# Two decode layers on one core: last wo and w2 blocks turned at once, sum of squares later, w3 as 3 and 2 rows, four V pages by halves of partitions

## The chip, the cores and the metric

The kernel runs on one core of a Trainium2 chip. The metric is the device time of one execution in microseconds (us), lower is better. A run of the program is timed several times; the median of the runs is the time that is compared.

## The reference

One token goes through attention and a gated feed-forward block, and through both once more with the same weights and the same caches. Each of the two passes is called a layer here.

```python
def _layernorm(x, eps=1e-5):               # no scale, no bias
    return (x - mean(x)) / sqrt(var(x) + eps)

def _A_ref(x, k_cache, v_cache, wq, wo):   # x: 1x1x640, caches: 32 heads x 32768 x 192, bf16
    W = min(4096, max(256, Sk // 4))       # 4096: the last 4096 positions are used
    q = (x @ wq) as 32 heads x 192
    p = softmax(q . k[last W] * 192 ** -0.5)
    return (p . v[last W]) @ wo            # wo: 6144x640

def _B_ref(x, w1, w3, w2):                 # w1, w3: 640x1536, w2: 1536x640
    return (silu(x @ w1) * (x @ w3)) @ w2

x = x + _A_ref(_layernorm(x), ...)
x = x + _B_ref(_layernorm(x), ...)
x = x + _A_ref(_layernorm(x), ...)
x = x + _B_ref(_layernorm(x), ...)
```

A head's 4096 x 192 keys are 1536 KB, its values as much, and there are 32 heads. A layer's caches and weights are over 100 MB, so nearly all of the work is to bring them in.

## The kernel before

All loads go out from SyncE (SP), in one order that the list `loads` (lines 192 to 235) sets down: for each layer wq in pieces, then pages of K and V by turns (V six heads behind K), then wo, w1, w3 and w2. Their destination is the `arena`, 32 units of 128 partitions x 3072 bf16 columns; a K or V page takes two units (128 partitions x 12288 bytes). `refill()` (lines 250 to 273) issues loads from the head of the list as long as `place()` finds free units; `done(key)` (line 289) frees the units of a page whose last reader has been written down, and refills. So the order of the program fixes which instruction a load waits for: the last reader of the units that it takes. The scheduler keeps eight semaphores for DMAs and takes them in turn, so a load also waits until the load eight places before it has landed. Three buffers lie outside the arena: `wo5` (the last 2560 columns of layer 0's wo), `keep` (the last 2400 of w2's 7680 columns, kept for layer 1) and `rest`.

Thirteen heads' K pages (`RETAIN`) stay in the arena from layer 0 to layer 1 and one more is parked in PSUM, so layer 1 loads fewer, and at the passage between the layers few units are free. There wq comes in ten pieces of 3072 columns, each of which can go out only when units are freed.

TensorE (PE) does the products with the weights, K or V as the moving operand; since x is one row, the stationary operand is narrow (32 columns for q, w1 and w3, one column for wo and w2). VectorE (DVE) turns each K page in blocks of 32x32 (line 379), finds the maxima of the softmax and sums; ScalarE (ACT) takes exponentials and copies.

The functions that the change touches, with their part in the order of work:

- `layernorm()` (lines 296 to 307): squares x on DVE, sums x and its squares by two fp32 products with a matrix of 1/640 (an fp32 product stands as two records on PE), subtracts the mean into `xs`, the stationary operand of what follows; the standard deviation's reciprocal `rstd` comes by Ln and Exp on ACT and is used only when a result is copied out of PSUM.
- `y_to_residual()` (309 to 319): the output of wo or w2 stands in PSUM as four partial rows of 640; ACT and DVE copy a half each to SBUF as `y_sb`, five products with `y_sb` as stationary operand turn and add them into a column per 128 elements, and DVE adds them to x (`xsq[:, 0:5]`).
- `wo_proj()` (491 to 521) multiplies blocks of 640 columns of wo (two matmuls of 320 columns) by one column of `otd`; `ffn()` (532 to 585) does w1, `gate()`, w3, the product and, in layer 0, w2 by blocks of 640 columns with a column of `htd`; `last_rows()` (587 to 598) does w2 in layer 1, straight into four rows of the output.
- `softmax_place()` (420 to 432) puts the turned probabilities of a block of four heads in place and forms the reciprocal of their sum; `combine()` (448 to 464) folds the block's output and scales it.
- `out_open()` and `out_residual()` (473 to 489) put x itself into the output's rows by five fp32 products.

A value is ready for the next part thus, at the passage from layer 0 to layer 1: last columns of w2 land in `keep`; their matmuls; both casts; five products; the residual; two fp32 sums; the subtraction; the first piece of wq; `done` of that piece, and with it the next load.

Of the kernel before, what the change touches and what calls it, by code (L numbers as in the profile page):

```python
# [8 lines left out]
F32 = mybir.dt.float32  # L9
# [6 lines left out]
P = 128  # L16
D = 640
# [23 lines left out]
SPLIT = (("k", 12),)  # L41
KW = 4 * HB
WH = 6 * KW + 32 - KW
KEEP = 2400
W2A = 2880
# [8 lines left out]
def kernel(  # L54
# [38 lines left out]
    onesD, rl, st, nv, lnv, rstd, l = (sc[:, a:b] for a, b in ((0, 1), (1, 2), (2, 4), (4, 5), (5, 6), (6, 7), (7, 8)))  # L93
# [8 lines left out]
    nc.vector.memset(xs[:].rearrange("p c n -> p (c n)").bitcast(U32), 0)  # L102
# [85 lines left out]

    def units_of(width):
        return -(-width // U)  # L190

    for layer in range(2):
# [3 lines left out]
        for i in range(H + LEAD):  # L196
            kinds = (("v", i - LEAD, A_v_cache), ("k", i, A_k_cache))
            for kind, g, cache in kinds[::-1] if k_first(layer, i) else kinds:
# [8 lines left out]
                if layer == 1 and (kind, h) in SPLIT:  # L207
                    for th in range(2):
                        loads.append(((kind, layer, h, th), 1, [(0, U, src[:, U * th:U * th + U])]))
                else:  # L210
                    loads.append(((kind, layer, h), 2, [(0, PGW, src)]))
        for key, ranges in wo_units(layer):
# [4 lines left out]
            if key:  # L217
                loads.append((key, units_of(at), parts))
            else:
                dst = wo5 if at == 2560 else wo4  # L220
                loads.append((None, None if dst is wo5 else LAST, [(dst[:, o:o + n], src) for o, n, src in parts]))
        if layer == 0:
# [7 lines left out]
            loads.append((None, None, [(keep[:], w2_v[:, 7680 - KEEP:7680])]))  # L230
        else:
            loads.append((("fa", layer), units_of(7680), [(0, 7680, w1_v[:, 0:7680])]))
            loads.append((("fb", layer), 2, [(0, PGW, w3_v[:, 0:PGW])]))
            loads.append((("fc", layer), 1, [(0, 1536, w3_v[:, PGW:])]))
# [15 lines left out]
    def refill():  # L250
        while loads:
# [18 lines left out]
            for off, w, src in parts:  # L270
                pin(nc.sync.dma_start(out=arena[:, s * U + off:s * U + off + w], in_=src))  # L271
# [24 lines left out]
    def layernorm():  # L296
        pin(nc.vector.tensor_tensor(out=xsq[:, 6:6 + NCH], in0=xsq[:, 0:NCH], in1=xsq[:, 0:NCH], op=ALU.mult))
        st_ps = m_ps[:, 0:12]
        for g in range(2):
            mm(st_ps[:, 6 * g:6 * g + 6], lhsT=onesD.broadcast_to([P, P]), rhs=xsq[:, 6 * g:6 * g + 6], start=True, stop=True)  # L300
        pin(nc.vector.reduce_sum(out=st[:, 0:1], in_=st_ps[:, 0:6], axis=AX.X))
        pin(nc.vector.tensor_scalar(out=xs[:, :, 3], in0=xsq[:, 0:NCH], scalar1=st[:, 0:1], scalar2=None, op0=ALU.subtract))
        pin(nc.vector.reduce_sum(out=st[:, 1:2], in_=st_ps[:, 6:12], axis=AX.X))
        pin(nc.vector.scalar_tensor_tensor(out=nv[:], in0=st[:, 0:1], scalar=st[:, 0:1], in1=st[:, 1:2],
                                           op0=ALU.mult, op1=ALU.subtract))
        pin(nc.scalar.activation(out=lnv[:], in_=nv[:], func=ACTF.Ln, scale=-1.0))
        pin(nc.scalar.activation(out=rstd[:], in_=lnv[:], func=ACTF.Exp, scale=-0.5))

    def y_to_residual(y_ps, f_ps=None):
# [4 lines left out]
        for c in range(NCH):  # L314
            mm(yt_ps[:, c:c + 1], lhsT=y_sb[:, c:D:NCH], rhs=onesb, start=True, stop=True)
# [22 lines left out]
    def q_turn(f0, f1, late):  # L338
# [7 lines left out]
        for a in range(4):  # L346
            dst = _ap(qt_sb[:], 0, 32, 96 * f0 + 2 * a, [[8, 2], [1, 2], [16, ns]])
            src = qt_ps[32 * a:32 * a + 32]
            eng = nc.vector if a % 2 and not late else nc.scalar
            pin((eng.copy if eng is nc.scalar else eng.tensor_copy)(out=dst, in_=src))  # L350
# [50 lines left out]
    def softmax_head(b, s_ps):  # L401
# [3 lines left out]
        for th in range(2):  # L405
# [9 lines left out]
                                 accum_out=l[0:64]))  # L415
# [4 lines left out]
    def softmax_place(b, et):  # L420
        engs = [nc.scalar, nc.vector, nc.scalar, nc.vector, nc.scalar, nc.vector, nc.scalar, nc.scalar]
        for th in range(2):
# [5 lines left out]
        half = slice(64 * (b % 2), 64 * (b % 2) + 64)  # L428
        rl_ps = m_ps[:, 0:1]
        mm(rl_ps[half], lhsT=lt[0:64], rhs=l[0:64], start=True, stop=True,  # L430
           tile_position=(0, 64 * (b % 2)))
        pin(nc.vector.reciprocal(out=rl[half], in_=rl_ps[half]))  # L432
# [15 lines left out]
    def combine(b, o_ps):  # L448
        half = slice(64 * (b % 2), 64 * (b % 2) + 64)
# [3 lines left out]
        ot_ps = m_ps.rearrange("p (q e) -> p q e", q=16)  # L453
        for par in range(2):
            mm(ot_ps[half].rearrange("p q e -> p (q e)"), lhsT=sel[:, par, :, :].rearrange("p h q -> p (h q)"),
               rhs=o_sb[:, 192 * par:192 * par + 192], start=(par == 0), stop=(par == 1),
               tile_position=(0, 64 * (b % 2)))
        om = w20[half, 384:576].rearrange("p (q e) -> p q e", q=16)
        pin(nc.vector.scalar_tensor_tensor(out=om, in0=ot_ps[half], scalar=rl[half],  # L459
                                           in1=mask[half].unsqueeze(2).broadcast_to([64, 16, 12]),  # L460
                                           op0=ALU.mult, op1=ALU.mult))
        with nc.allow_low_precision("one nonzero term in each sum"):
            pin(nc.vector.reduce_sum(out=otd[half, 12 * pos:12 * pos + 12], in_=om.rearrange("p q e -> p e q"),
                                     axis=AX.X))
# [8 lines left out]
    def out_open():  # L473
        assert not loads
        spare = free[0] * U
        ident = arena[:, spare:spare + 64].bitcast(F32)
        nc.gpsimd.memset(ident, 0.0)
# [3 lines left out]
        xw = arena[:, spare + 64:spare + 64 + 1280].bitcast(F32)  # L481
        nc.gpsimd.memset(xw, 0.0)
        for j in range(4):
            nc.gpsimd.tensor_copy(out=xw[32 * j:32 * j + 32, 32 * j:640:128], in_=xsq[32 * j:32 * j + 32, 0:NCH])
        return pss[:, 0:160], xw, ident

    def out_residual(f_ps, xw, ident):
        for c in range(NCH):
            mm(f_ps[:, c:160:NCH], lhsT=xw[:, 128 * c:128 * c + 128], rhs=ident, start=(c == 0), stop=False)

    def wo_proj(layer):
# [6 lines left out]
        for key, ranges in turns:  # L498
            at, width = 0, wo_width(ranges)
            for pos, lo, hi in ranges:  # L500
                x = lo
# [18 lines left out]
        y_to_residual(y_ps, last and last[0])  # L520
# [11 lines left out]
    def ffn(layer, f_ps):  # L532
# [20 lines left out]
        else:  # L553
            steps = ((g_ps, "fa", 0, 5, 0), (u_ps, "fb", 0, 4, 0), (u_ps, "fc", 4, 5, 0))
# [136 lines left out]
```

## Time and profile before

| what | value |
|---|---|
| median of three runs | 526.64 us (526.46 to 527.17) |
| profiled execution, device time | 525.68 us |
| profiled execution, span from first to last instruction | 523.7 us |
| mean granted clock of TensorE | 0.699 |
| bytes read | 219.74 MB, 420 GB/s over the span |
| busy share of the span: PE, DVE, ACT, POOL | 55%, 49%, 13%, 4% |
| loads of V pages | 64 of 1536 KB |
| loads of K pages of full width | 49 of 1536 KB |

"Span" is the time between the first and the last instruction of one profiled execution; the device time of the same execution holds some 2 us more. A row of the chain of waits says when a piece of the chain starts, how long it lasts, and which engine, tile and line it belongs to; "issue" is time in which an engine waited for nothing that the profile shows. Matmuls all stand at line 86, a helper, and are told apart by the tile that they write: q_ps, s_ps and o_ps in attention, y_ps for wo and w2, g_ps and u_ps for w1 and w3, pss for the small ones. In the busy windows a row gives a stretch of time, its length, each engine's busy time with the number of instructions, the granted clock, the share of the DMA engines' time and the rate.

### The profile page before, as it was taken

How to read it: one execution, taken by the hardware profiler on the slowest of the kernel's cores; microseconds unless marked ns; L12 is line 12 of the kernel's file. 1: busy time of each engine (PE TensorE's matmuls, PEld its weight loads, DVE VectorE, ACT ScalarE, POOL GpSimd, SP SyncE). 2: the span in 40 equal slices, each digit the busy share in tenths (PEclk: the TensorE clock that was granted, in tenths of full speed). 3: DMA queues.
4: the chain of work that ended last, by engine and by line, in shares of the span. 5: the costliest groups of instructions: out<-in, count | busy, mean ns of one | idle time of the engine just before them, and what ended most of it. 6: DMA issues, size and time to landing. Idle time of an engine off the chain costs nothing.

```text
span 523.7 us, 5996 instructions
## 1 busy us (share of the span) xinstructions
PE 286.0 (55%) x2396; PEld 111.3 (21%) x2396; DVE 255.8 (49%) x385; ACT 66.0 (13%) x202; POOL 19.1 (4%) x86
## 2 busy tenths in 40 slices
PE   3335555463655544655555685676356565365564
PEld 1101222121222111212112231232112222122132
DVE  0079885656746476763002117431678565565002
ACT  1010210110202020202001022121201120112000
POOL 4010000000000000000000001000000000001000
PEclk9967778675776768666555577788557867776567
DMA  9999999999999999999999999999999999999996
GB/s 376 406 432 428 428 431 428 429 429 429 429 430 428 431 429 427 430 429 429 424 420 403 388 412 433 428 426 431 426 432 430 426 432 426 431 431 427 431 428 251
DMA packets 22931, 220.12 MB, mean 420 GB/s; under 512 B 2680, under 2 KB 3064, under 8 KB 7288
## 3 DMA queue, kind: packets, MB, share of 16 engines
q1 hardware_dynamic: 22760, 219.75, 99.2%
q8 instruction: 19, 0.31, 0.2%
q14 instruction: 8, 0.07, 0.0%
q10 hardware_dynamic: 144, 0.00, 0.0%
HBM read 219.74 MB, written 0.00 MB: 420 GB/s over the span
## 4 chain that ended last, share of the span: by engine, by line
DMA 84%; PE 10%; DVE 3%; issue 1%; ACT 1%; SPq 1%; DVEq 0%; ACTq 0%
DMA arena<-in_A_k_cache_dram 47%; DMA arena<-in_A_v_cache_dram 24%; DMA arena<-in_B_w_dram 6%; PE s_ps L86 5%; PE o_ps L86 2%; DVE arena L379 2%; DMA arena<-in_A_wo_dram 2%; DMA keep<-in_B_w_dram 2%; DMA arena<-in_A_wq_dram 1%; DMA wo<-in_A_wo_dram 1%; PE q_ps L86 1%; PE pss L86 1%; SPq L271 1%; PE u_ps L86 0%; PE y_ps L86 0%
## 5 line engine op out<-in xcount | busy, mean ns | idle before, releaser
L86 PE MATMUL s_ps<-arena,wst 128*16 128x512 bf16 (+1 forms) x768 | 157.7, 524 | 157.4 <-DVE arena L379 80.7
L379 DVE STREAM_TRANSPOSE arena<-arena 128x1536 uint32<-128x1536 uint32 x100 | 171.1, 1753 | 67.0 <-DMA arena<-in_A_k_cache_dram 66.5
L86 PE MATMUL o_ps<-arena,ptm 128*8 128x384 bf16 (+1 forms) x1024 | 115.2, 438 | 24.0 <-DMA arena<-in_A_v_cache_dram 24.0
L86 PEld LDWEIGHTS <-wst 128*16 128x16 bf16 (+1 forms) x768 | 48.9, 108 | 248.3 <-issue 216.1
L86 PEld LDWEIGHTS <-ptm 128*8 128x8 bf16 (+1 forms) x1030 | 40.7, 102 | 65.1 <-issue 53.4
L411 ACT ACTIVATE nt<-m 32x16 f32<-32x16 f32 x16 | 3.4, 213 | 271.4 <-DVE m L408 271.4
L427 ACT COPY ptm<-w 32x64 bf16<-32x64 bf16 x80 | 23.6, 295 | 46.5 <-PE o_ps L86 44.2
L86 PE MATMUL q_ps<-arena,xs 128*32 128x512 bf16 x120 | 19.2, 589 | 13.4 <-DMA arena<-in_A_wq_dram 12.3
L363 POOL COPY wst<-qt_sb 32x24 bf16<-32x24 bf16 x30 | 8.4, 280 | 422.9 <-PE s_ps L86 307.1
L459 DVE SCALAR_TENSOR_TENSOR w<-pss,sc,cb 64x192 bf16<-64x192 f32 x16 | 6.7, 416 | 33.5 <-PE pss L86 33.5
L402 DVE TENSOR_REDUCE lt<-s_ps 64x1 f32<-64x512 f32 x16 | 10.9, 684 | 23.0 <-PE s_ps L86 22.6
L86 PE MATMUL y_ps<-arena,otd 128*1 128x320 bf16 x176 | 15.3, 438 | 9.8 <-DMA arena<-in_A_wo_dram 9.3
L417 DVE STREAM_TRANSPOSE w<-w 64x512 bf16<-64x512 bf16 x16 | 11.3, 705 | 14.4 <-ACT w L414 14.4
L312 DVE CAST w<-y_ps 128x320 bf16<-128x320 f32 x3 | 1.5, 491 | 30.6 <-PE y_ps L86 30.6
L350 DVE CAST qt_sb<-pss 32x48 bf16<-32x48 f32 (+1 forms) x4 | 1.2, 307 | 28.6 <-ACT qt_sb L350 28.6
L86 PEld LDWEIGHTS <-xs 128*32 128x32 bf16 x200 | 8.3, 114 | 32.0 <-issue 25.2
L427 DVE COPY ptm<-w 32x64 bf16<-32x64 bf16 x48 | 10.0, 209 | 10.0 <-PE o_ps L86 8.9
L432 DVE RECIPROCAL sc<-pss 64x1 f32<-64x1 f32 x16 | 2.6, 165 | 23.1 <-PE pss L86 22.9
L452 ACT CAST w<-o_ps 128x384 bf16<-128x384 f32 x16 | 7.7, 479 | 31.8 <-PE o_ps L86 24.9
L414 ACT ACTIVATE w<-s_ps,nt 64x512 bf16<-64x512 f32 x16 | 10.9, 682 | 5.7 <-DVE nt L412 5.7
L86 PE MATMUL pss<-w,sel 128*64 128x192 bf16 x32 | 6.3, 286 | 8.1 <-ACT w L452 5.1
L86 PEld LDWEIGHTS <-otd 128*1 128x1 bf16 x192 | 5.8, 102 | 20.3 <-issue 15.8
(81 smaller groups left out, 119.2 us busy)
## 6 DMA issues: line engine op xcount, KB each, us to landing
arena<-in_A_v_cache_dram SPq DMA_DIRECT2D x64, 1536.0 KB, 29.2
arena<-in_A_k_cache_dram SPq DMA_DIRECT2D x49, 1536.0 KB, 29.2
arena<-in_A_wq_dram SPq DMA_DIRECT2D x10, 768.0 KB, 6.7
arena<-in_A_wq_dram SPq DMA_DIRECT2D x1, 4608.0 KB, 20.0
arena<-in_A_wo_dram SPq DMA_DIRECT2D x6, 720.0 KB, 8.7
arena<-in_A_wo_dram SPq DMA_DIRECT2D x2, 1920.0 KB, 30.1
arena<-in_A_wq_dram SPq DMA_DIRECT2D x2, 1536.0 KB, 7.7
arena<-in_B_w_dram SPq DMA_DIRECT2D x4, 768.0 KB, 7.1
```

What stands on the lines that cost most here:

```text
L86: return pin(nc.tensor.matmul(*a, **k))
L271: pin(nc.sync.dma_start(out=arena[:, s * U + off:s * U + off + w], in_=src))
L363: pin((engs[a].copy if engs[a] is nc.scalar else engs[a].tensor_copy)(out=dst, in_=src))
L379: pin(nc.vector.transpose(x, x))
L402: pin(nc.vector.reduce_max(out=t0[:, 0:1], in_=s_ps[0:64, :], axis=AX.X))
L411: pin(nc.scalar.mul(out=tb[32:64, 0:KW].rearrange("p (a z) -> p a z", a=4), in_=mb, mul=-SCALE))
L414: pin(nc.scalar.activation(out=e[:], in_=s_ps[0:64, :], func=ACTF.Exp, bias=nbt[:, 0:1], scale=SCALE, accum_out=l[0:64]))
L417: pin(nc.vector.transpose(et[:], e[:]))
L427: pin((eng.copy if eng is nc.scalar else eng.tensor_copy)(out=dst, in_=src))
L432: pin(nc.vector.reciprocal(out=rl[half], in_=rl_ps[half]))
L452: pin(nc.scalar.copy(out=o_sb[:, 0:384], in_=o_ps[:, 0:384]))
L459: pin(nc.vector.scalar_tensor_tensor(out=om, in0=ot_ps[half], scalar=rl[half], in1=mask[half].unsqueeze(2).broadcast_to([64, 16, 12]), op0 ...
```

## The change

- Layer 0's last 1920 columns of wo (`wo5`) and of w2 (`keep`) are three blocks of 640. They are no longer multiplied as the moving operand with a column of `otd` or `htd`, copied and turned. Each block itself, in five sets of 128 columns, is the stationary operand, and the column of `otd` or `htd` the moving one, so that the result is turned as it comes and adds to the same PSUM columns as the turned rest. The loads of `wo5` and `keep` are cut in three (`tail_cuts`): what lies ahead of the last two blocks in two transfers, and the last two blocks (1280 columns) in one.
- `layernorm()` does the sum of x and the subtraction, and returns `spread()`, which does the sum of squares and `rstd`; it is called after the first piece of wq, or after the first row of w1.
- Layer 1's w3 comes as 4608 and 3072 columns (3 and 2 of its 5 rows) in place of 6144 and 1536.
- Layer 1's V pages of heads 28 to 31, the last four, are loaded as two transfers each, of partitions 0 to 63 and 64 to 127 (`ROWS`).
- Fewer or other instructions: one sum and one reciprocal for two blocks of the softmax; `combine()` on partitions 0 to 63 for every block; all copies of the turned q on ACT; the copy of u on ACT in place of DVE; x into the output by one fp32 product of 160 columns in place of five of 32; the first memsets of `xs` and `wst` on GpSimd.

```diff
+ROWS = (28, 29, 30, 31)
+TAIL = 3 * 640
...
-    onesD, rl, st, nv, lnv, rstd, l = (sc[:, a:b] for a, b in ((0, 1), (1, 2), (2, 4), (4, 5), (5, 6), (6, 7), (7, 8)))
+    onesD, rl, st, nv, rstd, lnv, l = (sc[:, a:b] for a, b in ((0, 1), (1, 3), (3, 5), (7, 8), (5, 6), (6, 7), (6, 8)))
...
+    def tail_cuts(width):
+        return (0, width - TAIL), (width - TAIL, 640), (width - 1280, 1280)
...
-                    loads.append(((kind, layer, h), 2, [(0, PGW, src)]))
+                    parts = [(0, PGW, src)]
+                    if layer == 1 and kind == "v" and h in ROWS:
+                        parts = [(0, PGW, src[p0:p0 + 64], p0) for p0 in (0, 64)]
+                    loads.append(((kind, layer, h), 2, parts))
...
+                if dst is wo5:
+                    src = parts[0][2]
+                    parts = [(o, n, src[:, o:o + n]) for o, n in tail_cuts(2560)]
...
-            loads.append((None, None, [(keep[:], w2_v[:, 7680 - KEEP:7680])]))
+            loads.append((None, None, [(keep[:, o:o + n], w2_v[:, 7680 - KEEP + o:7680 - KEEP + o + n])
+                                       for o, n in tail_cuts(KEEP)]))
...
-            loads.append((("fb", layer), 2, [(0, PGW, w3_v[:, 0:PGW])]))
-            loads.append((("fc", layer), 1, [(0, 1536, w3_v[:, PGW:])]))
+            loads.append((("fb", layer), 2, [(0, 4608, w3_v[:, 0:4608])]))
+            loads.append((("fc", layer), 1, [(0, 3072, w3_v[:, 4608:])]))
...
-            for off, w, src in parts:
-                pin(nc.sync.dma_start(out=arena[:, s * U + off:s * U + off + w], in_=src))
+            for off, w, src, *at in parts:
+                p0 = at[0] if at else 0
+                pin(nc.sync.dma_start(out=arena[p0:p0 + src.shape[0], s * U + off:s * U + off + w], in_=src))
...
-        for g in range(2):
+
+        def total(g):
             mm(st_ps[:, 6 * g:6 * g + 6], lhsT=onesD.broadcast_to([P, P]), rhs=xsq[:, 6 * g:6 * g + 6], start=True, stop=True)
-        pin(nc.vector.reduce_sum(out=st[:, 0:1], in_=st_ps[:, 0:6], axis=AX.X))
+            pin(nc.vector.reduce_sum(out=st[:, g:g + 1], in_=st_ps[:, 6 * g:6 * g + 6], axis=AX.X))
+
+        total(0)
         pin(nc.vector.tensor_scalar(out=xs[:, :, 3], in0=xsq[:, 0:NCH], scalar1=st[:, 0:1], scalar2=None, op0=ALU.subtract))
...
+        def spread():
+            total(1)
...
+        return spread
...
-        for c in range(NCH):
-            mm(yt_ps[:, c:c + 1], lhsT=y_sb[:, c:D:NCH], rhs=onesb, start=True, stop=True)
+        turned_y = (lambda c: y_sb[:, c:D:NCH], onesb)
+        parts = [turned_y]
+        if tail:
+            w, hid, lo = tail
+            parts = [(lambda c, k=k: w[:, 640 * k + c:640 * k + 640:NCH], hid[:, lo + k:lo + k + 1]) for k in range(3)]
+            parts.insert(1, turned_y)
+            mm(yt_ps, lhsT=ptm[:, 2:3].broadcast_to([P, P]), rhs=ptm[:, 0:NCH], start=True, stop=False)
+        for n, (lhsT, rhs) in enumerate(parts):
+            for c in range(NCH):
+                mm(yt_ps[:, c:c + 1], lhsT=lhsT(c), rhs=rhs, start=not tail, stop=(not tail or (n, c) == (len(parts) - 1, NCH - 1)))
...
-        half = slice(64 * (b % 2), 64 * (b % 2) + 64)
-        rl_ps = m_ps[:, 0:1]
-        mm(rl_ps[half], lhsT=lt[0:64], rhs=l[0:64], start=True, stop=True,
-           tile_position=(0, 64 * (b % 2)))
-        pin(nc.vector.reciprocal(out=rl[half], in_=rl_ps[half]))
+        if b % 2:
+            rl_ps = m_ps[0:64, 0:2]
+            mm(rl_ps, lhsT=lt[0:64], rhs=l[0:64], start=True, stop=True)
+            pin(nc.vector.reciprocal(out=rl[0:64], in_=rl_ps))
...
-    def out_residual(f_ps, xw, ident):
-        for c in range(NCH):
-            mm(f_ps[:, c:160:NCH], lhsT=xw[:, 128 * c:128 * c + 128], rhs=ident, start=(c == 0), stop=False)
+    def out_residual(f_ps, xw, blk):
+        mm(f_ps, lhsT=blk, rhs=xw, start=True, stop=False)
...
-            steps = ((g_ps, "fa", 0, 5, 0), (u_ps, "fb", 0, 4, 0), (u_ps, "fc", 4, 5, 0))
+            steps = ((g_ps, "fa", 0, 5, 0), (u_ps, "fb", 0, 3, 0), (u_ps, "fc", 3, 5, 0))
...
+                if ps is g_ps and c == 0:
+                    spread()
...
-        pin(nc.vector.tensor_scalar(out=gu[:, 1, :], in0=u_ps[:, 0:384], scalar1=rstd, scalar2=None, op0=ALU.mult))
+        pin(nc.scalar.mul(out=gu[:, 1, :], in_=u_ps[:, 0:384], mul=rstd))
...
-        for fcx in range(12):
+        for fcx in range(9):
...
-        y_to_residual(y_ps)
+        y_to_residual(y_ps, None, (keep[:, KEEP - TAIL:], htd, 9))
...
             q_piece(layer, piece, q_ps)
+            if piece is now[0]:
+                spread()
```

## The prediction

> **What bounds the kernel now.** I read the 40 slices and the chain of waits on the page, then the busy windows by stage, then the chain in order of time at the two places that the change names.
>
> ```profile
> GB/s 376 406 432 428 428 431 428 429 429 429 429 430 428 431 429 427 430 429 429 424 420 403 388 412 433 428 426 431 426 432 430 426 432 426 431 431 427 431 428 251
> ...
> DMA 84%; PE 10%; DVE 3%; issue 1%; ACT 1%; SPq 1%; DVEq 0%; ACTq 0%
> ...
> arena<-in_A_v_cache_dram SPq DMA_DIRECT2D x64, 1536.0 KB, 29.2
> ```
>
> The DMA engines are busy in every slice, at 426 to 433 GB/s but for the start, slices 20 to 24 (the passage from layer 0 to layer 1) and the end. A page of K or V (1536 KB, 1.573 MB) therefore costs 1.573/0.430 = 3.66 us, and is issued 29.2 us ahead. The time is bytes over rate, plus the start, the dips and the tail; whatever lies beside the stream is free.
>
> ```profile
> 440.00:460.00 20.00, 9.70 (x73) 3.57 (x71) 11.39 (x14) 1.56 (x5) 0.56 (x2) 0.67 1.01 431
> ...
> 268.00:276.00 8.00, 4.55 (x50) 0.96 (x42) 0.00 (x0) 0.00 (x0) 0.00 (x0) 0.50 1.03 426
> ...
> 296.00:297.00 1.00, 0.97 (x8) 0.28 (x6) 0.00 (x0) 0.00 (x0) 0.00 (x0) 0.50 0.76 209
> 297.00:298.00 1.00, 0.39 (x2) 0.00 (x0) 0.00 (x0) 0.00 (x0) 0.00 (x0) 0.50 0.80 246
> ...
> 517.00:518.00 1.00, 1.00 (x17) 0.48 (x15) 0.40 (x2) 0.18 (x1) 0.00 (x0) 1.00 0.81 326
> 518.00:519.00 1.00, 0.47 (x6) 0.00 (x0) 0.66 (x3) 0.00 (x0) 0.00 (x0) 1.00 0.50 197
> 519.00:520.00 1.00, 0.53 (x23) 0.45 (x27) 0.32 (x2) 0.00 (x0) 0.00 (x0) 1.00 0.19 72
> ```
>
> The columns are the stretch, its length, busy time of PE, PEld, DVE, ACT and POOL, the granted clock, the DMA share and GB/s. Two things are to be seen. At 296 to 298 the stream runs dry: (425-209)+(425-246) = 395 GB/s-us, or 395/425 = 0.93 us lost. And at the end the rate fades over three microseconds: the 16 DMA engines, each with 1/16 of the bytes, do not finish together but over some 2.5 us.
>
> ```profile
> 290.86 0.77 PE y_ps L86 x8
> 291.63 0.02 issue
> 291.65 0.50 DVE w L312
> 292.15 0.14 issue
> 292.29 0.35 PE pss L86 x5
> ...
> 292.87 1.03 PE pss L86 x4
> 293.91 0.02 issue
> 293.93 0.18 DVE sc L301
> ```
>
> This is why it runs dry. The last w2 block lands at 290.81; product, cast, turn, residual, two fp32 sums and the subtraction end at 294.37, and only after the first wq piece (six matmuls, 1.05 us) is a page of the arena free, at 295.5, for the next load.
>
> ```profile
> 516.28 0.87 PE u_ps L86 x5
> ...
> 517.32 1.17 PE u_ps L86 x6
> ...
> 518.52 0.63 DVE w L566
> ...
> 519.71 1.03 PE pss L86 x48
> ```
>
> The tail: w3's four rows land at 516.24, and 4.5 us of work follow until 520.74; the last w2 transfer, issued at 499.1 with 21.2 us to landing, comes in at 520.3, so only 0.4 us of that is more than waiting for data.
>
> **The change, part by part.** *The passage.* After keep's last transfer only two of its blocks are left to turn: 10 products of the kind that took 0.35/5 = 0.07 each, 0.70; then the residual 0.02+0.17+0.04, one fp32 sum in place of two (1.03/2 = 0.52), reduce and subtract 0.02+0.18+0.02+0.24: 1.91 us in place of 3.51. The casts of y and the first block's turn lie ahead of the landing. 1.6 us is more than the 0.93 that the stream loses, so the gain is 0.93; the bounds are 0.5 (if the extra transfers eat into it) and 1.1 (with the 0.15 us missing at 299 to 300). What is late next: the second sum (0.52) now stands on PE behind the first wq piece, so the second piece is done 1.6-0.5 = 1.1 us sooner than before, still ahead of its need. The same shortening after wo, 1.6 less the 0.52 that now stands between the w1 rows, meets the dip at 281 to 283 ((425-324)+(425-295), 0.54 us); there one engine was behind the others and did not wait, as the next blocks' matmuls wait for landings (1 and 2 us) all the same. I take 0, bound 0.54.
>
> *More transfers.* wo5 and keep come as 3 each: four more issues of 0.33 us on SP, where w1 (270.46) and wq (285.30) wait for PE until later anyway; uncovered they would cost 1.3 us. Rows are 960 to 2560 B. The last three transfers of before, back to back, took 0.80 us for 320 KB and 0.52 for 200 KB between first landings, 0.04 over bytes at 430 GB/s; six such less the two replaced (0.06): +0.18, bounds 0 and 0.3. [...]
>
> *w3 as 3 and 2 rows.* The first three rows (1152 KB) land 384 KB, 0.9 us, sooner, at 515.3; the last two at 517.16 as before. After that, eight matmuls (0.87), the copy now on ACT (0.58, as L543 has it, for 0.62), turn and product 0.3+0.25, to 519.25; then 48 products that wait for the last landing, 520.32, with five left (0.11) and 0.06 of latency: 520.53 for 520.74. Gain 0.21, bounds 0 and 0.4.
>
> *Fewer instructions.* One reciprocal and one sum for two blocks, the residual as 1 fp32 product for 5 (at 502, where PE then waits 3.00 us for wo), memsets and qt copies on other engines: all lie beside the stream with 29.2 us of loads ahead. 0. Without that cover a reciprocal on DVE behind two 1.75 us transposes would hold PE's combine, and the v products behind it, 3.5 us.
>
> *Four V pages in halves.* The diff's other edit (ROWS) loads the last four V pages of layer 1 as 64 partitions and 64 partitions, eight transfers for four; four more issues, 29 us ahead, cost nothing, and eight halves in flight hold 14.6 us of work. No row shows a load into fewer than 128 partitions. Low end: by bytes, 1.83 us a half, 0 in all. High end: by what partitions have been seen to take. No stage brings a partition more than 431/128 = 3.4 GB/s; to cost nothing, 64 partitions would have to take 6.7 each, twice anything that any row shows. At 3.4 a half lasts as long as a page, 3.66 us, and four pages cost 4 x 3.66 = 14.6 us more. Which row is nearest? Partitions of 12288 B at 3.66 us: it is the same row of 12288 B, with half the partitions left out. So I take the high mechanism, less one relief: the engines are out of step by up to 2.5 us, so of two that now write into one group of eight partitions (16 engines, 8 groups in a half) one may be in the second half while the other is in the first. A pair with a lead s collides only for 1.83-s of each half, and the pair with the least lead ends last; eight pairs over 2.5 us leave one at about 0.4: 8 x (1.83-0.4) = 11.4 us. Bounds of the relief: least lead 0 (14.6) and 0.9 (7.4).
>
> [...]
>
> Sum: -0.93 + 0.18 - 0.21 + 11.4 = **+10.4**. Against the profiled execution: span 523.7 to 534.1, with the 2.0 us around it 525.68 to 536.1; the median of the runs is 0.96 above that execution, so 526.64 to **537.1**.
>
> **Rivals.** *The halves are free* (an engine's own pace, not the partitions', sets 430 GB/s). For it: each engine keeps its pace when the others stand idle, and a transfer of half the bytes (768 KB) takes half the time in the passage. Against: those still use all partitions. Then the rest stands: -0.96, 525.7, between 525.0 and 526.4. This is the other side: it holds from the point where a half takes under 1.95 us (8 x 0.12 = 0.96).
>
> *Halves free, passage not gained*: the next load waits for something else than the first wq piece, as a page that the later pieces free, and the dip only moves. For: the arena is nearly full of kept K pages there. Against: 295.5 is when that piece ends and the dry stretch follows at once. +0.18-0.21: 526.6.
>
> *Halves free, PE behind*: the shared reciprocal holds combine. For: DVE is busy 11.39 of 20 us with transposes. Against: PE has half its time free. In the stretch of kept K pages (315 to 330, PE busy 10 of 15 us) one hold of 3.5 us less some 0.5 of slack: +3-0.96, about 528.7.
>
> **How the numbers follow.** Likeliest, 0.65: 537.1, its own range 532.6 to 540.5 (the relief's bounds and half a microsecond of the rest). Halves free 0.26, half of it under 525.6; passage not gained 0.05; PE behind 0.04. Bounds of 0.2% (1.05 us), about what a measurement of this kernel can tell from no change: faster 0.13, same 0.13+0.05 = 0.18, slower 0.65+0.04 = 0.69. The range takes in the halves' being free: 525.1 to 540.3.
>
> **What would show it.** Right: in windows over the last V pages (from about 482) a rate near 240 to 280 GB/s for some 26 us; no dip behind the last w2 block; PE's last product within 0.25 us of the last landing. Wrong: 430 GB/s there throughout, which makes the first rival true; a dip that stays though the sums came sooner; or dips at stretches where PE waits for the reciprocal.

## The result, and the profile after

| what | before | after |
|---|---|---|
| median of the runs | 526.55 us (524.83 to 527.17) | 540.54 us (539.69 to 543.42) |
| profiled execution, device time | 525.68 us | 540.94 us |
| profiled execution, span | 523.7 us | 539.2 us |
| loads of V pages | 64 of 1536 KB | 60 of 1536 KB, 8 of 768 KB |
| busy share of the span: PE, DVE | 55%, 49% | 52%, 47% |

The changed kernel is slower: its time is 1.0275 [1.0247, 1.0303] of that of before, 14.0 us more. The direction is the one that was forecast, and the loss lies where the forecast put it, over the last V pages; the time is 3.4 us above the forecast (537.1 us) and 0.24 us above the top of its range.

From the page of the kernel after: the rate in 40 slices of 13.48 us, and the loads of V with KB each and median us from issue to landing.

```profile
GB/s 365 421 428 431 428 428 429 430 428 427 431 426 432 427 432 428 431 428 430 418 413 408 385 419 428 427 430 428 431 428 429 431 428 430 428 328 222 264 430 245
...
arena<-in_A_v_cache_dram SPq DMA_DIRECT2D x60, 1536.0 KB, 29.2
...
arena<-in_A_v_cache_dram SPq DMA_DIRECT2D x8, 768.0 KB, 30.1
```

The row of rates is that of before but for three slices near the end: 328, 222, 264. The halves were issued 30.1 us ahead, so they were in the queue in time. The busy windows of the kernel after at this place (stretch, length, busy time of PE, PEld, DVE, ACT and POOL with numbers of instructions, granted clock, DMA share, GB/s):

```profile
472.00:476.00 4.00, 0.95 (x6) 0.30 (x3) 3.36 (x2) 0.00 (x0) 0.00 (x0) 0.93 1.00 427
476.00:480.00 4.00, 3.48 (x27) 1.35 (x27) 1.12 (x4) 0.00 (x0) 0.00 (x0) 0.63 1.08 356
480.00:484.00 4.00, 1.08 (x18) 0.67 (x18) 2.22 (x10) 2.35 (x8) 1.64 (x9) 0.80 1.00 218
...
492.00:496.00 4.00, 0.28 (x4) 0.10 (x8) 0.00 (x0) 0.00 (x0) 0.00 (x0) 0.50 1.03 228
...
504.00:508.00 4.00, 0.19 (x4) 0.00 (x0) 0.00 (x0) 0.00 (x0) 0.00 (x0) 0.50 1.03 217
508.00:512.00 4.00, 1.17 (x16) 0.39 (x16) 0.00 (x0) 0.00 (x0) 0.00 (x0) 0.50 0.94 353
512.00:516.00 4.00, 2.98 (x36) 1.26 (x36) 0.90 (x2) 0.48 (x1) 0.00 (x0) 0.50 1.00 430
```

Two columns matter. The rate falls to about half (217 to 228 GB/s) while the DMA share stays at 1.00 to 1.03: the engines are not idle, each packet takes about twice as long. A packet of 12288 bytes took 460 ns in the median from 440 to 460 us, and 894 from 484 to 504. PE does next to nothing meanwhile (0.28 of 4 us): it waits for V.

When the 16 parts of a transfer landed (the trace's semaphore events; us from the span's start):

```
whole page, last but one   first 473.84   last 476.26
whole page, last           first 477.49   last 481.48
first half                 first 480.49   last 485.18
second half                first 483.99   last 488.68
third half                 first 487.48   last 492.18
...
eighth half                first 504.96   last 510.79
```

A half takes 3.50 us, nearly as long as a page (3.66). From 476.26 to 510.79 one whole page and four halved ones came in: 34.53 us, where five whole pages take 18.28. That is 16.25 us more at the landings. Up to the last whole page but one, the two executions are level: it landed at 476.26, before at 476.21. So nothing had been gained in the 476 us that hold the passage.

The passage itself, in the order of PE's work (start, us, tile and operands, and in brackets the idle time with what ended it):

```profile
291.46 0.54 PE L88 MATMUL pss<-htd,keep 128*128 128x1 bf16 x10
292.25 0.59 PE L88 MATMUL pss<-xsq,sc 128*128 128x6 f32 x2 [0.25 <-DVE xsq L347]
293.37 1.04 PE L88 MATMUL q_ps<-arena,xs 128*32 128x512 bf16 x6 [0.53 <-DVE xs L318]
294.34 0.59 PE L88 MATMUL pss<-xsq,sc 128*128 128x6 f32 x2
294.86 1.04 PE L88 MATMUL q_ps<-arena,xs 128*32 128x512 bf16 x6
296.57 1.04 PE L88 MATMUL q_ps<-arena,xs 128*32 128x512 bf16 x6 [0.67 <-DMA arena<-in_A_wq_dram]
298.40 1.04 PE L88 MATMUL q_ps<-arena,xs 128*32 128x512 bf16 x6 [0.78 <-DMA arena<-in_A_wq_dram]
```

The first wq piece starts at 293.37, 1.05 us sooner than before (294.42). But the third now waits for its own landing, 296.53, where before three pieces (18 matmuls) ran in one go. The row of the kernel before:

```profile
294.42 2.97 PE L86 MATMUL q_ps<-arena,xs 128*32 128x512 bf16 x18 [0.53 <-DVE sc L303]
```

The busy windows of the kernel before, then of the kernel after, same columns as above:

```profile
294.00:296.00 2.00, 1.58 (x12) 0.67 (x13) 0.61 (x4) 0.41 (x2) 0.00 (x0) 0.50 1.05 439
296.00:298.00 2.00, 1.35 (x8) 0.28 (x6) 0.00 (x0) 0.00 (x0) 0.00 (x0) 0.50 0.78 227
298.00:300.00 2.00, 1.04 (x6) 0.28 (x6) 0.00 (x0) 0.00 (x0) 0.00 (x0) 0.50 0.98 387
300.00:302.00 2.00, 1.04 (x6) 0.13 (x5) 0.00 (x0) 0.00 (x0) 0.00 (x0) 0.50 1.01 409
```

```profile
294.00:296.00 2.00, 1.90 (x10) 0.78 (x9) 0.39 (x2) 0.41 (x2) 0.00 (x0) 0.50 0.99 415
296.00:298.00 2.00, 1.04 (x6) 0.28 (x6) 0.00 (x0) 0.00 (x0) 0.00 (x0) 0.50 0.93 329
298.00:300.00 2.00, 1.04 (x6) 0.27 (x6) 0.00 (x0) 0.00 (x0) 0.00 (x0) 0.50 0.93 292
300.00:302.00 2.00, 1.04 (x6) 0.13 (x5) 0.00 (x0) 0.58 (x1) 0.00 (x0) 0.50 0.99 387
```

The dip is shallower and two microseconds longer; the mean over the eight is 366 before and 356 after. The dip moved, and is no smaller.

One execution differs from the next, so a longer stretch over all traces tells more: from the 108th to the 140th megabyte read, which holds the dips of both kernels. With the passage of before it took 77.52 us (before) and 77.96 (halves_only, below), with that of after 77.58 to 78.07 in thirteen traces, 77.82 in the mean.

The end, by the chain of waits of the kernel after:

```profile
515.09 20.82 DMA arena<-in_B_w_dram
535.95 0.31 PE pss L88 x5
```

The last product ends 0.35 us behind the last landing; before it was 0.42 (520.32 to 520.74).

### The profile page after: what moved, and what is told of

The parts are those of the page before. It is cut to its first block, busy times and chain, and to the rows that moved or that the text cites. A ratio compares the mean times of both kernels' runs of the same rounds, so it can differ in the third digit from the quotient of the medians.

```text
span 539.2 us, 5997 instructions
## 1 busy us (share of the span) xinstructions
PE 280.5 (52%) x2392; PEld 109.8 (20%) x2392; DVE 252.1 (47%) x369; ACT 68.4 (13%) x208; POOL 19.4 (4%) x88
## 4 chain that ended last, share of the span: by engine, by line
DMA 90%; PE 6%; DVE 2%; issue 0%; ACT 0%; SPq 0%; ACTq 0%; DVEq 0%
DMA arena<-in_A_k_cache_dram 45%; DMA arena<-in_A_v_cache_dram 29%; DMA arena<-in_A_wo_dram 8%; DMA arena<-in_B_w_dram 5%; PE s_ps L88 3%; DMA arena<-in_A_wq_dram 3%; PE o_ps L88 2%; DVE arena L406 1%; PE q_ps L88 1%; PE y_ps L88 1%; PE pss L88 0%; SPq L284 0%; PE g_ps L88 0%; PE u_ps L88 0%; ACT w L441 0%
## 5 line engine op out<-in xcount | busy, mean ns | idle before, releaser
L88 PE MATMUL q_ps<-arena,xs 128*32 128x512 bf16 x120 | 18.9, 572 | 13.4 <-DMA arena<-in_A_wq_dram 12.2
L390 DVE COPY wst<-qt_sb 32x24 bf16<-32x24 bf16 x4 | 1.1, 276 | 25.7 <-ACT qt_sb L377 25.7
L88 PE MATMUL pss<-xsq,sc 128*128 128x6 f32 x16 | 4.8, 370 | 8.2 <-ACT xsq L105 7.3
## 6 DMA issues: line engine op xcount, KB each, us to landing
arena<-in_A_v_cache_dram SPq DMA_DIRECT2D x8, 768.0 KB, 30.1
```

The source lines that it names most:

```text
L88: return pin(nc.tensor.matmul(*a, **k))
L390: pin((engs[a].copy if engs[a] is nc.scalar else engs[a].tensor_copy)(out=dst, in_=src))
```

## The experiments

Ratios are to the kernel before, run beside each kernel on the same chip, with 95% intervals. Diffs are against the kernel after unless said otherwise.

### The halves alone, and all but the halves

*no_halves*: `ROWS = ()`, everything else as after. *halves_only*: the kernel before, with the rows of the diff on `ROWS` and `parts` alone.

> The changed kernel with the last four V pages loaded whole again; all else of the change stays. Theory (partitions): the halves alone made it slower. Between the same points of the two traces (landing of the page ahead of the four, landing of the fourth) the changed kernel took 34.5 us for what takes 18.3 at 3.66 us a page, 16.2 more; without it the span should be 539.2 - 16.2 = 523.0, the time about 525 to 526.5, and the rate over the last V pages 430 GB/s. Rival (the rest of the change costs too, say the sum of squares between the wq pieces): over 527, with the dip after the last w2 block deeper than before.

> The kernel before, with nothing of the change but the last four V pages in two transfers of 64 partitions. Theory (partitions): the whole loss is here, +14 to +16 us, 541 to 543, and the rate over these pages 215 to 240 GB/s for about 28 us. Rival (the halves hurt only together with the other edits, by the order of loads or the eight semaphores): under 530.

Measured: no_halves 525.93 us, 0.9993 [0.998, 1.0006]; halves_only 542.81 us, 1.0312 [1.0297, 1.0328]. The whole loss is that of the halves, and all other edits together make no difference that the times can tell (their interval is -1.05 to +0.3 us). Both ways to price the halves: 540.54 - 525.93 = 14.6 us on top of the other edits, 542.81 - 526.4 = 16.4 on top of the kernel before. Of the 1.8 us between the two, the landings show 0.4 ahead of the halves (476.65 against 476.26), 0.5 in them (35.05 against 34.53) and 0.9 behind them. Why the two differ stays open.

From the page of no_halves, the rate in 40 slices:

```profile
GB/s 373 412 428 429 430 429 428 431 427 432 429 428 431 428 428 432 428 426 433 423 411 412 374 416 427 431 429 426 432 429 429 429 427 432 430 427 429 433 426 256
```

Every slice near the end, but for the last, is back at 426 to 433.

### Is it the size of the transfers, or the partitions?

*column_halves* cuts the same four pages into as many transfers of the same bytes, but each over all 128 partitions:

```diff
-                        parts = [(0, PGW, src[p0:p0 + 64], p0) for p0 in (0, 64)]
+                        parts = [(o, U, src[:, o:o + U]) for o in (0, U)]
```

> The changed kernel, but the four pages are cut in two by columns: two transfers of all 128 partitions and 3072 columns each, the same bytes and the same number of transfers as the halves of partitions. Theory (partitions): no loss, as without the halves, 525 to 526.5. Rival (more transfers, rows of 6144 B, fewer bytes in flight behind eight semaphores): the loss stays, 535 to 541.

Measured: 525.83 us, 0.9995 [0.9983, 1.0007]. Two of its busy windows:

```profile
480.00:484.00 4.00, 1.52 (x21) 0.49 (x17) 2.66 (x12) 1.92 (x7) 2.17 (x10) 0.93 1.02 426
484.00:488.00 4.00, 2.62 (x30) 1.22 (x34) 0.99 (x3) 1.01 (x3) 0.00 (x0) 0.50 1.01 419
```

Twice as many transfers of half the size cost nothing. It is the partitions.

### How much per page, and how much at the seams

*two_pages*: `ROWS = (30, 31)`.

> The changed kernel with halves for the last two V pages only. Theory (each half lasts 3.5 us, and entering and leaving the halves costs some 2.8 us once): 4 x 1.68 + 2.8 = 9.5 us over whole pages, 534 to 536. Rival (no cost at the seams, 16.2 us shared evenly by four pages): 8.1 us, 533 to 534.5. The seams are read from the landings in the trace, since the times lie close.

Measured: 533.79 us, 1.0147 [1.013, 1.0165]: 7.7 us over the kernel before, 7.9 over no_halves. The theory (534 to 536) is missed, the rival (533 to 534.5) holds. The last V page landed at 502.95, without halves at 494.8: 8.2 us later, where four pages are 16.0 later (510.79). Over no_halves four pages cost 14.6, so two more pages add 14.6 - 7.9 = 6.7 by the times, or 3.4 a page (2 x 3.50 - 3.66 is 3.34), and 7.8 by the landings, or 3.9 a page; 1.2 or 0.4 us is left to be paid once, on going into the halves and out of them. The loss grows with the pages; how much of it is paid once, these runs don't fix.

*early_halves* moves the halves to heads 16 to 19 of layer 0, where each halved V page stands between whole K pages:

```diff
-ROWS = (28, 29, 30, 31)
+ROWS = (16, 17, 18, 19)
...
-                    if layer == 1 and kind == "v" and h in ROWS:
+                    if layer == 0 and kind == "v" and h in ROWS:
```

> The changed kernel with halves for four V pages in the first third of layer 0, heads 16 to 19, in place of the last four of layer 1. Theory (no lead of one engine over another relieves the halves): the same loss as at the end, +13.5 to +15, 539 to 541.5. Theory of the prediction (engines that are out of step get out of each other's way): early on they land within 0.5 us of each other in place of 2.4, so the loss is larger by up to 8 x 0.3 = 2.4 us, 542 to 543.5. If it is below 537, loads that wait ahead in the queue hide a part of it at this place.

Measured: 550.63 us, 1.0457 [1.0415, 1.0499]. Both expectations are missed. At this place (104 to 150 us) the 16 parts of a whole page land over 1.6 to 1.7 us in the trace of the kernel after, not 0.5 as was expected. Its busy windows over these pages:

```profile
104.00:112.00 8.00, 5.38 (x40) 1.82 (x36) 4.96 (x7) 1.95 (x6) 0.00 (x0) 0.77 0.99 211
112.00:120.00 8.00, 0.83 (x16) 0.42 (x17) 0.05 (x1) 0.00 (x0) 0.00 (x0) 0.66 1.02 247
120.00:128.00 8.00, 3.77 (x20) 1.07 (x24) 3.39 (x2) 0.00 (x0) 0.00 (x0) 0.50 0.97 241
```

The rate is low throughout, though half of the pages in this stretch are whole K pages: those between halves take 6.2 to 6.3 us from the last landing ahead to their own. Halves slow the whole pages next to them. So the loss is 24.4 / 4 = 6.1 us for each halved page that stands between whole ones, and 14.6 / 4 = 3.65 where four stand together.

### Other ranges of partitions

*middle_half* takes each page as partitions 32 to 95, then 0 to 31, then 96 to 127; *rows_96_32* as 0 to 95 and 96 to 127; *sixteen_rows* the last page alone (`ROWS = (31,)`) as eight transfers of 16 partitions.

```diff
-                        parts = [(0, PGW, src[p0:p0 + 64], p0) for p0 in (0, 64)]
+                        parts = [(0, PGW, src[p0:p0 + n], p0) for p0, n in ((32, 64), (0, 32), (96, 32))]
```

> The changed kernel, but each of the four pages comes as partitions 32 to 95, then 0 to 31, then 96 to 127. Theory by count (each partition takes 3.4 GB/s at most, so a transfer lasts 3.5 us whatever partitions it has): 3 x 3.5 = 10.5 us a page, +6.8 x 4 = 27 us over whole pages, about 553. [...]

> The changed kernel with each of the four pages as partitions 0 to 95 and 96 to 127. Theory flat: both at 225 GB/s, 7.0 us a page as with halves, 539 to 542. [...]

> The changed kernel, but only the last V page of layer 1 is cut, into eight transfers of 16 partitions. Theory flat (any transfer that does not span all 128 partitions moves at 225 GB/s, wherever it goes; so it was for 64, and for 32 to 95, 0 to 31 and 96 to 127): 7.0 us for the page, +3.4 and a seam of 0.9, 530 to 531.5. [...]

Measured: middle_half 538.28 us, 1.024 [1.0192, 1.0289]; rows_96_32 541.84 us, 1.0287 [1.0255, 1.0319]; sixteen_rows 531.57 us, 1.0096 [1.0069, 1.0122]. One busy window each, in this order:

```profile
488.00:492.00 4.00, 1.47 (x16) 0.47 (x16) 0.00 (x0) 0.00 (x0) 0.00 (x0) 0.50 0.99 200
```

```profile
492.00:496.00 4.00, 0.00 (x0) 0.00 (x0) 0.00 (x0) 0.00 (x0) 0.00 (x0) 0.50 0.98 203
```

```profile
492.00:496.00 4.00, 1.45 (x16) 0.39 (x15) 0.00 (x0) 0.00 (x0) 0.00 (x0) 0.50 0.92 197
```

All three run at about 190 to 245 GB/s while their pieces flow. In rows_96_32 the 1152 KB for 0 to 95 took 5.2 to 5.9 us and the 384 KB for 96 to 127 some 1.85, which is 6.6 GB/s for each of these 32 partitions. So the price is not by the number of partitions, which is what the forecast's high mechanism supposed. For middle_half the theory by count fell (553 us expected); for the other two the flat rate held (sixteen_rows 0.07 us above its range).

The other two runs say less of a single range, since several of their transfers are under way at once. In middle_half the parts of one transfer land over some 7 us, as long as a whole page takes there; in sixteen_rows over 5 us, with a new transfer every 0.9 us. And the first 32 to 95 of middle_half, straight behind a whole page, had its first part 1.85 us behind the page's, where later ones took 3.2 to 3.6. Whether 32 to 95, or 16 partitions, are slow by themselves is not shown.

### Neighbours, sides, or rows of memory

*even_odd* takes each page as its even partitions and then its odd ones:

```diff
-                        parts = [(0, PGW, src[p0:p0 + 64], p0) for p0 in (0, 64)]
+                        parts = [(0, PGW, src[p0:P:2], p0) for p0 in (0, 1)]
...
-                pin(nc.sync.dma_start(out=arena[p0:p0 + src.shape[0], s * U + off:s * U + off + w], in_=src))
+                pin(nc.sync.dma_start(out=arena[slice(p0, P, 2) if at else slice(0, P), s * U + off:s * U + off + w], in_=src))
```

> The changed kernel with each of the four pages as the even and the odd partitions, 64 each, both spread over the whole of 0 to 127. Theory flat: as the halves, 3.5 us a transfer, 539 to 542. [...]

Measured: 561.42 us, 1.0666 [1.0635, 1.0698], slower than every kernel above and far from the 539 to 542 us of the flat theory, and yet the windows over its first halves show the full rate, 433 and 427 GB/s at 476 to 484. The time goes elsewhere. The waits of SP's queue in even_odd behind 460 us (waiting line, what it waited for, us in total, times, longest):

```profile
SPq L284 <- DVE arena L406: 46.8, 2, 25.0
```

Line 406 turns K pages in the arena. In the kernel after, the same loads have no such wait; in even_odd the scheduler lets them wait for these turns, so that loads go out late and the queue runs dry. A transfer of 64 partitions at full rate ends the theory that a partition, or 64 of them, take no more. But in even_odd the rows read from memory are parted too. *far_rows* keeps the neighbouring partitions and parts the rows; *near_rows* is even_odd with neighbouring rows.

```diff
-                        parts = [(0, PGW, src[p0:p0 + 64], p0) for p0 in (0, 64)]
+                        parts = [(0, PGW, src[p0 // 64:P:2], p0) for p0 in (0, 64)]
```

> Changed beside the kernel after: each half of the last four V pages still writes 64 neighbouring partitions (0 to 63, then 64 to 127), but reads every second row of the page in memory instead of 64 neighbouring rows. So the V rows of these four pages stand in another order than the reference's, and the output with them; bytes, waits and instructions are the same. Theory: the 64 neighbouring partitions are the narrow place: a half still lasts 3.4 to 3.6 us, 215 to 245 GB/s over the four pages, 539 to 542 us. Rival: the 64 neighbouring rows of memory are the narrow place: a half lasts 1.8 to 1.9 us, 420 to 433 GB/s, 525.5 to 527 us.

> Changed beside the kernel after: each half of the last four V pages reads 64 neighbouring rows of memory, as there, but writes every second partition. So the V rows of these four pages stand in another order than the reference's, and the output with them. The loads wait for readers of the arena as in even_odd, so its total time tells little (555 to 565 us where the transfers are fast, some 15 us more where they are slow); read is the rate while the first four halves flow, about 472 to 484 us. Theory (partitions): 1.8 to 1.9 us a half, 420 to 433 GB/s. Rival (rows of memory): 3.4 to 3.6 us a half, 215 to 245 GB/s.

Measured: far_rows 540.35 us, 1.0276 [1.0243, 1.0309], the time of the kernel after; near_rows 560.62 us, 1.0661 [1.063, 1.0692]. Two busy windows of far_rows, then two of near_rows:

```profile
484.00:488.00 4.00, 0.48 (x2) 0.13 (x1) 0.90 (x2) 0.48 (x2) 0.68 (x3) 0.50 0.99 215
...
500.00:504.00 4.00, 1.17 (x16) 0.38 (x16) 0.00 (x0) 0.00 (x0) 0.00 (x0) 0.50 0.96 215
```

```profile
476.00:480.00 4.00, 0.00 (x0) 0.00 (x0) 0.00 (x0) 0.00 (x0) 0.00 (x0) 0.50 1.00 427
480.00:484.00 4.00, 0.00 (x0) 0.00 (x0) 0.00 (x0) 0.00 (x0) 0.00 (x0) 0.50 1.03 439
```

Where the rows lie in memory made no difference in these runs; which partitions are written did. The landings say the same: 3.5 us a half in far_rows, 1.83 in near_rows.

What about them? *low_steps* takes a page as four transfers of 32 partitions: the even ones of 0 to 63, the odd ones, and both again for 64 to 127. *quarter_steps* takes every fourth partition of all 128.

```diff
+                        parts = [(0, PGW, src[sl], sl) for sl in [slice(o + e, o + 64, 2) for o in (0, 64) for e in (0, 1)]]
...
+                        parts = [(0, PGW, src[sl], sl) for sl in [slice(e, P, 4) for e in range(4)]]
```

> The last four V pages come as four transfers each, of 32 partitions: every second one of 0 to 63, the others of 0 to 63, and the same for 64 to 127. Theory: what is narrow is the side of memory, so that partitions 0 to 63 alone give half the rate however the partitions are picked: 215 to 245 GB/s in four-us windows while these transfers flow. Rival: what is narrow is neighbouring partitions, and leaving out every second one relieves it: 400 to 433 GB/s. The loads wait for readers of the arena, so the total says little (more than 555 us by both).

> The last four V pages come as four transfers each, of 32 partitions: every fourth one of all 128. Theory: what counts is that a transfer reaches over the whole range of partitions, not how many it writes: 420 to 433 GB/s while they flow. Rival: a partition takes no more than the 6.7 GB/s of even_odd (430 GB/s over 64 partitions): 32 of them take 215 GB/s. The loads wait for readers of the arena, so the total says little (more than 555 us by both).

Measured, one run each: 575.84 and 563.32 us (before 526.06), with the waits of even_odd in both (42.9 and 30.4 us for the turns of K pages). The windows, low_steps first:

```profile
480.00:484.00 4.00, 0.00 (x0) 0.00 (x0) 0.00 (x0) 0.00 (x0) 0.00 (x0) 0.50 1.02 227
484.00:488.00 4.00, 0.00 (x0) 0.00 (x0) 0.00 (x0) 0.00 (x0) 0.00 (x0) 0.50 0.96 215
```

```profile
476.00:480.00 4.00, 0.00 (x0) 0.00 (x0) 0.00 (x0) 0.00 (x0) 0.00 (x0) 0.50 1.02 433
480.00:484.00 4.00, 0.00 (x0) 0.00 (x0) 0.00 (x0) 0.00 (x0) 0.00 (x0) 0.50 1.00 424
```

The same 32 partitions' worth of bytes goes at 215 to 227 GB/s when it stays within 64 partitions and at 424 to 433 when it reaches over all 128. So it is neither the number of partitions nor that they are neighbours, but where they lie. Of all patterns tried, those that reach over all 128 (whole pages, column_halves, even_odd, near_rows, quarter_steps) took the full rate, 419 to 439 GB/s in the windows above, and those that stay within 0 to 63 or 64 to 127 about half of it (the halves 217 to 228, low_steps 215 to 227). But 0 to 95, which reach over both sides of 64, took about half of it too: 1152 KB in 5.2 to 5.9 us, 200 to 227 GB/s.

What stays open is why 0 to 95, lying on both sides, are slow as well. No run shows how the 16 engines share out the rows of such a transfer.

### The passage

Three kernels without halves (`ROWS = ()`). *squares_third*: layer 1's sum of squares after the third wq piece in place of the first. *squares_at_once*: the sum of squares where it was before, ahead of the first piece. *moving_tail*: `wo5` and `keep` loaded whole and multiplied as the moving operand, as before, with the sum of squares late.

```diff
-            if piece is now[0]:
+            if piece is now[2 if layer else 0]:
...
-        return spread
+        spread()
+        return lambda: None
...
-        y_to_residual(y_ps, None, (keep[:, KEEP - TAIL:], htd, 9))
+        y_to_residual(y_ps)
```

> The changed kernel without halves, and in layer 1 the sum of squares stands behind the third wq piece, not the first. Theory (in the changed kernel the dip only moved: the sixth wq load waits for the second piece, which the sum of squares on the matrix engine put off by 0.45 us): the second piece's load goes out 0.45 us sooner, the dip at 296 to 300 shrinks from about 1.1 us to 0.6, and the time falls by 0.4 to 0.5 us against the kernel with whole pages. Rival (the sixth load was late for another reason, its start on the DMA engines): no difference within 0.1 us.

> The changed kernel without halves, and the sum of squares again ahead of what uses x. Theory (one fp32 sum, 0.5 us, stands ahead of the first wq piece instead of behind it; the second piece's load goes out as late as in the changed kernel): the fifth wq load 0.5 us later, the sixth the same, so the time rises by 0 to 0.5 us against the kernel with whole pages. Rival (the later sum is what gains at the passage): it rises by the full 0.5 to 0.6 us.

> The changed kernel without halves, and with layer 0's last wo and w2 blocks multiplied as the moving operand and turned afterwards, as before; the loads of these blocks whole. Theory (standing weights shorten the way from the last w2 block to the first wq piece by 1.1 us: 10 products for 8 matmuls, a cast and 5 products): the dip grows by 1.1 us less what the smaller rows cost (0.2), so the time is 0.5 to 1 us above the kernel with whole pages. Rival (the passage is bound elsewhere and the turn at once is worth nothing): the same within 0.2 us or below.

Measured: squares_third 525.87 us, 0.9999 [0.9989, 1.0009]; squares_at_once 525.69 us, 0.9991 [0.9979, 1.0002]; moving_tail 526.77 us, 1.0009 [0.9997, 1.0021]. Against no_halves (525.93) the place of the sum of squares makes no difference that these runs can tell: the intervals reach some 0.5 us either way, and so much was expected. moving_tail's median is 0.84 us higher, but the two intervals overlap. From the 108th to the 140th megabyte moving_tail took 78.47 us, more than any other trace (squares_third 77.76, squares_at_once 77.56). So it is likely, but on one trace, that the standing weights, with their loads in three, gain some 0.65 us over moving ones once the sum of squares is late; over the kernel before they gain nothing. Where squares_third's dip went (busy windows of squares_third):

```profile
298.00:300.00 2.00, 1.23 (x7) 0.47 (x8) 0.38 (x2) 0.41 (x2) 0.00 (x0) 0.50 1.02 406
300.00:302.00 2.00, 1.04 (x6) 0.13 (x5) 0.00 (x0) 0.56 (x1) 0.00 (x0) 0.50 0.99 320
302.00:306.00 4.00, 2.77 (x20) 1.10 (x22) 0.42 (x2) 1.44 (x6) 1.11 (x4) 0.50 0.97 379
```

298 to 300 is mended (406, after: 292), and 300 to 306 pays for it (320 and 379, after: 387 and 417). The dip moves on a second time.

## Why the prediction was right and wrong

**The halves: the right part and sign, a wrong reason, short in size.** The forecast took the high mechanism, a half as long as a page, 14.6 us for four pages, less a relief of 3.2. The half took 3.50 us, so that the four cost 8 x 3.50 - 4 x 3.66 = 13.4 by this alone; 14.6 to 16.4 were measured in all. Three things failed.

- *The relief by the engines' leads*, -3.2 us (14.6 to 11.4). It supposed that an engine that runs ahead writes into the other half and meets nobody; which partitions an engine writes was the author's estimate, and no run shows it. The 16 parts of a half land over 4.7 us, more than a half lasts, so nearly all engines had leads; yet from the second half on the first part of each also comes 3.50 us after the first part of the half ahead. The early engines are as slow as the late ones. The relief measured nothing, but for 0.5 us of the first half's lead (480.49 - 477.49 = 3.00).
- *The seams were not in the sum.* Going into the halves, the whole page ahead took 5.22 us in place of 3.66, the first half 3.70 and the last 4.58 (506.21 to 510.79), in place of 3.50: 1.56 + 0.20 + 1.08 = 2.8 us that no term held, and 13.4 + 2.8 is the 16.25 of the landings. Of this 15.5 is left at the last load (535.91; 520.39 in no_halves). The size of the seams varies, as two_pages shows. early_halves shows the same at its largest, whole K pages of 6.3 us beside halves.
- *The reason given for the high mechanism*, that a partition takes no more than 3.4 GB/s, was wrong: in even_odd 64 partitions took 430 GB/s, 6.7 each, and in quarter_steps 32 took 13.4 each. That it gave a nearly right number was luck: the halves ran at about half the rate (217 to 228 GB/s), and a half has half the bytes.

The prediction's own terms also don't all come out. "No stage brings a partition more than 431/128" overlooks the start, where the windows of the kernel before show 482 GB/s at 10 to 13 us, 3.8 a partition. The top of the range, 540.3, is the sum without any relief; with the half microsecond that the low end has it would be 540.8. And 520.32 + 0.11 + 0.06 is 520.49, not 520.53.

**The passage: forecast -0.93, nothing in the traces.** The chain behind `keep` did shorten, if less than worked out: from its last landing to `xs` it took 2.28 us (291.04 to 293.32), not 1.91, because the cast of y ended behind the landing (290.63 + 0.49) and its five products stood ahead of the last ten. With the landing 0.23 later, the first piece started 1.05 us sooner, not 1.6. The step that failed is the next one: "the second piece is done 1.6-0.5 = 1.1 us sooner than before, still ahead of its need". It was done 0.4 us sooner, and the need lay elsewhere: the next two loads went out sooner (294.45 for 295.50, 295.94 for 296.35), but the third and fourth later (297.64 for 297.42, 299.47 for 299.23), because their wq pieces waited for landings of their own, which came some 0.2 us later than before (296.53 for 296.31, 298.36 for 298.12). The half K page behind the wq pieces landed at 312.40 in both kernels. This is the mechanism of the second rival, that the dip only moves, which had 0.05. A stall was costed by its deepest two microseconds, without following the loop: units freed by a piece, a load into them, some 7 us to landing, the next piece. That the loop with its few free units sets the rate there is argued from these times; no run had more units.

**More transfers: +0.18, measured +0.23** at the last landing of `keep` (290.81 to 291.04) in these two traces; others with the same transfers have it at 290.93 to 291.49. **The tail: -0.21, measured -0.07.** The last product ends 0.35 us behind the last landing, where 0.25 was the sign of being right. It does follow the landing, but the five products left took 0.31 us, not 0.11: they wait for the landing and then run as their own small group. **Fewer instructions: 0, held**: the rate in no_halves is 426 to 433 in every slice but for the start, the passage and the end, and no hold of PE shows in it, so the third rival (a shared reciprocal) fell. **The dip at 281 to 283: 0 taken, held**, though the dip itself did fill: the windows at 280 to 284 have 362 GB/s before, 419 after and 401 in no_halves. What it gave was lost again behind it (292 to 294: 409 before, 369 and 381), a second case of a dip that moves. The rest sums to -0.96 in the forecast, and no_halves gave 525.93 for 526.4, an interval from -1.05 to +0.3 us. The times alone leave the -0.96 just possible; the 77.5 to 78.1 us of the stretch around the passage, the same with the old and the new one, do not.

**Halves free**, the rival on the other side, fell with the rate of 217 to 228 GB/s.

## What to carry to other kernels

A load that is cut should be cut along the bytes of a partition and not across the partitions: column_halves cost nothing, halves of the same size 14.6 us, and they slow the whole transfers beside them too (5.2 to 6.3 us for 3.66). Where a stream runs dry at a passage, follow the loop of freed buffer, load, landing and next use once round before booking the gain; a step that comes sooner may only meet the next one's wait. A full DMA share at half the GB/s was here the sign of slow packets (894 ns for 460) and not of late loads.

## What the runs showed that was not expected

- 32 partitions spread over all 128 take the full rate (424 to 433 GB/s), 96 neighbouring ones about half of it (203 in one window).
- A load to every second partition made the scheduler wait for readers of other pages: 46.8 us of waits on SP in even_odd, 35 us in its time. The fast way to write 64 partitions made a kernel 21 us slower than the slow way.
- A whole page next to pieces of fewer partitions takes 5.2 to 6.6 us in place of 3.66 (6.6 ahead of the pieces of sixteen_rows).
- A half lasts 3.50 us and not 3.66: 225 GB/s is a little more than half of 430.
